# Splitting the last token tile of the last feed-forward into two halves of its output features

## Chip, cores and metric

One Trainium2 chip, one of its cores; the sets of experiments ran on three different chips, each with runs of the kernel before beside them. The metric is device microseconds of one execution; lower is better. Beside it I use a finer measure that comes from the traces: the time from the start of the last token tile's first matmul (called t = 0 in this document) to later points of the same execution. Two executions of the same program agree on it to a few ns as far as the end of computing, while whole times of one program scatter by 1 to 2 us (nine runs of the kernel before on one chip span 1.3 to 1.8).

## The reference, cut to what matters

A Conformer block on x of 2 x 4000 x 512: feed-forward, attention, convolution, a second feed-forward, and a final layer normalization. The change is in the last two lines:

```python
h = _layernorm(x3, axis=-1)
h = _silu(h @ w_ff2_a) @ w_ff2_b      # 512 -> 2048 -> 512
x4 = x3 + 0.5 * h
return _layernorm(x4, axis=-1)
```

## The kernel before

Tokens come in 16 chunks of 500, a chunk in four tiles (TPC = 4) of 125 tokens. The second product of the feed-forward has for each tile 16 matmuls (FC = 16), whose stationary operand is a 128 x 125 block of activations and whose moving operand is a 128 x 512 block of weights; they accumulate in one bank of PSUM, the accumulator memory. In the last chunk the four tiles are done one after the other, so that each tile's epilogue (residual, statistics, normalization, store) runs while TensorE is at the next tile. The last tile has no next one.

```python
def ff_last(self, c, old):
    ...                                     # first product of all 16 blocks
    sl = self.nxt("ln", self.LN_SLOTS)
    for ti in range(TPC):
        for f in range(FC):
            self.ff_second(f, ti, *blocks[f], f == FC - 1)        # 128x125 by 128x512, PE
        self.residual(self.Yb[ti][0:TILE, :], self.b_Y[ti], c * TPC + ti, 0.5)   # DVE, reads PSUM
        self.ln_stats(c, sl, ti)                                  # DVE, bn_stats
        self.ln_mean(sl, ti)                                      # DVE, bn_aggr
        self.ln_factor(sl, ti)                                    # DVE add eps, then POOL power -0.5
        self.ln_norm(c, sl, ti, self.osb[0][:, ti, :], self.b_osb[0][ti], "DVE")
        self.store_out(c, self.osb[0], self.b_osb[0], ti, ti + 1, ("SP", "ACT"))  # 80 and 45 rows
```

Every operation goes through a helper that notes which buffers it reads and writes and puts the semaphore waits in front of it; a `Buf` stands for what is tracked as one. The program uses semaphores as counters: an operation that is done adds one to its engine's, and an engine that needs the result waits for that value. The order in which the program lists VectorE's operations is the order in which the traces show them (e1_order below tests it: there residual 1, listed earlier, starts at t = 1.95 instead of 3.02). In the lines of the profile PE is TensorE and PEld its weight loads, DVE is VectorE, POOL is GpSimd, ACT is ScalarE, and SPq is the queue of SyncE.

Of the kernel before, what the change touches and what calls it, by code (L numbers as in the profile page):

```python
# [8 lines left out]
ALU = mybir.AluOpType  # L9
# [3 lines left out]
B, T, D, F, KW = 2, 4000, 512, 2048, 3  # L13
TILE = 125
CHUNK = 500
TPC = CHUNK // TILE
# [6 lines left out]
FC = F // 128  # L23
# [195 lines left out]
class Conformer:  # L219
# [484 lines left out]
    def ff_last(self, c, old):  # L704

        S, late = self.S, FC - self.NP
        blocks = []
        for f in range(FC):
            if f < late:
                blocks.append((self.late[f], self.b_late[f]))  # L710
            else:
                s = self.nxt("P", self.NP)
                blocks.append((self.P[s], self.b_P[s]))
            self.ff_first(c, f, *blocks[f])
            self.pop({0: old // 2, 1: old - old // 2}.get(f, 0))
            self.tick()
        while self.later:
            self.tick()
        sl = self.nxt("ln", self.LN_SLOTS)
        for ti in range(TPC):  # L720
            for f in range(FC):
                self.ff_second(f, ti, *blocks[f], f == FC - 1)
            self.residual(self.Yb[ti][0:TILE, :], self.b_Y[ti], c * TPC + ti, 0.5)
            self.ln_stats(c, sl, ti)
            self.ln_mean(sl, ti)
            self.ln_factor(sl, ti)
            self.ln_norm(c, sl, ti, self.osb[0][:, ti, :], self.b_osb[0][ti], "DVE")
            self.store_out(c, self.osb[0], self.b_osb[0], ti, ti + 1, ("SP", "ACT"))
# [720 lines left out]
```

## Time and profile before

| | before |
|---|---|
| device time, median of 4 runs | 2061.34 us (2060.94 to 2062.01) |
| span in the profile | 2056.9 us |
| TensorE busy | 2044.4 us |
| t = 0 (first matmul of the last tile) | at 2047.75 us |
| last matmul ends | t = 3.62 |
| aggregate of the last tile ends | t = 5.29 |
| normalization ends | t = 6.56 |
| end of the span | t = 9.20 |

The table reads as follows: nothing but the 5.58 us from 3.62 to 9.20 lies open behind TensorE, and 2.64 of these are the last store. Two more lines of before matter later, and neither was used in the prediction. First the page's row of instruction fetches (packets, MB, share of the DMA engines), then, from the waits of SyncE over the last microseconds (total us, times, longest), its wait for the stores to land:

```profile
q8 instruction: 77, 1.26, 0.3%
```
```profile
SPq L178 <- DMA out_dram<-work: 1.3, 2, 0.9
```

### The profile page before, as it was taken

What the parts mean: (1) busy time and instruction counts of PE and PEld (TensorE: products, weight loads), DVE (VectorE), ACT (ScalarE), POOL (GpSimd) and SP (SyncE); (2) the same over time, 40 slices, a digit from 0 to 9 for tenths busy, and PEclk for the clock granted to TensorE, in tenths of its full rate; (3) what the DMA queues carried; (4) which work ended last, traced back from release to release, by engine and by line L of the source; (5) the groups of instructions that cost most, each with busy time, mean ns of one, the idle gap of its engine ahead of it and who ended that gap; (6) DMA issues with size and microseconds to landing.
All of it is one profiled execution on the core that took longest, in us unless ns stands there. A gap on an engine that the chain in (4) does not pass through costs nothing.

```text
span 2056.9 us, 24335 instructions
## 1 busy us (share of the span) xinstructions
PE 2044.4 (99%) x9625; PEld 1036.1 (50%) x9625; DVE 1111.3 (54%) x2274; ACT 744.6 (36%) x1270; POOL 128.1 (6%) x275
## 2 busy tenths in 40 slices
PE   9999999999999999999999999999999999999998
PEld 4555555554444444444444444444445555555554
DVE  4245444325556667666666676667764443443443
ACT  3433333333333333333333333333345443443432
POOL 2011100000000000000000000000011000000000
PEclk9999999999999999999999999999999999999999
DMA  7222221110000100014301000101143111111111
GB/s 178 56 61 56 58 61 49 46 49 11 16 6 23 24 16 18 21 23 110 92 17 24 18 23 14 23 18 24 39 127 93 31 31 41 31 31 41 31 31 42
DMA packets 209323, 87.71 MB, mean 43 GB/s; under 512 B 157873, under 2 KB 208692, under 8 KB 209204
## 3 DMA queue, kind: packets, MB, share of 16 engines
q1 hardware_dynamic: 208808, 85.79, 16.7%
q8 instruction: 77, 1.26, 0.3%
q14 instruction: 42, 0.34, 0.1%
q10 hardware_dynamic: 396, 0.31, 0.0%
HBM read 29.53 MB, written 19.04 MB: 24 GB/s over the span
## 4 chain that ended last, share of the span: by engine, by line
PE 96%; DVE 2%; SPq 1%; DMA 1%; issue 0%; POOL 0%; ACT 0%; POOLq 0%; DVEq 0%; ACTq 0%
PE s L465 54%; PE y L465 42%; SPq L515 1%; DMA xt<-in_x_dram 1%; DMA work<-in_dw_dram 0%; DVE work L547 0%; SPq L511 0%; DVE work L569 0%; DVE wff L1048 0%; DVE xt L667 0%; SPq L519 0%; POOL work L661 0%; POOL work L1057 0%; DVE wff L953 0%; ACT work L507 0%
## 5 line engine op out<-in xcount | busy, mean ns | idle before, releaser
L507 ACT ACTIVATE work<-s 128x500 bf16<-128x500 f32 (+2 forms) x1063 | 623.7, 587 | 1220.4 <-PE s L465 1218.9
L465 PE MATMUL s<-work,wff 128*128 128x500 bf16 x2560 | 627.7, 376 | 1.7 <-DVE work L504 1.7
L465 PE MATMUL s<-work,keys 128*128 128x500 bf16 x2048 | 517.5, 374 | 0.1
L465 PE MATMUL y<-work,keys 128*128 128x500 bf16 x2048 | 514.4, 373 | 0.1
L465 PE MATMUL y<-wff,work 128*125 128x512 bf16 x2016 | 506.6, 379 | 0.0
L820 DVE TENSOR_TENSOR work<-work 128x500 f32<-128x500 f32 x496 | 334.8, 675 | 281.9 <-ACT work L507 279.1
L465 PEld LDWEIGHTS s<-work,wff 128*128 128x128 bf16 x2560 | 250.1, 98 | 280.9 <-issue 1.8
L465 PEld LDWEIGHTS y<-wff,work 128*125 128x125 bf16 x2016 | 275.2, 137 | 173.5
L465 PEld LDWEIGHTS y<-work,keys 128*128 128x128 bf16 x2048 | 199.2, 97 | 234.4 <-DVE work L885 1.1
L465 PEld LDWEIGHTS s<-work,keys 128*128 128x128 bf16 x2048 | 199.8, 98 | 232.2 <-DVE work L749 0.6
L667 DVE SCALAR_TENSOR_TENSOR xt<-y,xt 125x512 bf16<-125x512 f32 x128 | 79.8, 684 | 342.0 <-PE y L465 342.0
L547 DVE BATCH_NORM_STATS2 work<-xt 125x6 f32<-125x512 bf16 x316 | 199.8, 681 | 10.4 <-DMA xt<-in_x_dram 10.2
L556 POOL TENSOR_TENSOR work<-work 125x4 f32<-125x4 f32 x76 | 77.0, 1013 | 1116.6 <-DVE work L554 1116.6
L465 PE MATMUL s<-work 128*125 128x512 bf16 (+3 forms) x528 | 133.7, 378 | 2.2 <-DVE work L1158 1.2
L569 DVE TENSOR_SCALAR work<-xt,work 125x512 bf16<-125x512 bf16 x279 | 113.0, 449 | 16.5 <-POOL work L556 12.9
L667 DVE SCALAR_TENSOR_TENSOR xt<-s,xt 125x512 bf16<-125x512 f32 x56 | 38.8, 692 | 146.3 <-PE s L465 146.3
L465 PEld LDWEIGHTS s<-work 128*125 128x125 bf16 (+2 forms) x528 | 70.5, 135 | 48.1 <-issue 2.7
L667 DVE SCALAR_TENSOR_TENSOR xt<-s,work,xt 125x512 bf16<-125x512 f32 x64 | 48.1, 751 | 32.5 <-PE s L465 31.9
L465 PE MATMUL s<-keys,work 128*128 128x500 bf16 x256 | 64.4, 376 | 0.0
L957 DVE SCALAR_TENSOR_TENSOR wff<-wff,s 128x500 bf16<-128x500 f32 x57 | 38.6, 678 | 43.5 <-PE s L465 41.4
L507 ACT ACTIVATE wff<-s 128x500 f32<-128x500 f32 x67 | 39.2, 587 | 57.2 <-PE s L465 55.1
L507 ACT ACTIVATE work<-keys,work 128x500 bf16<-128x500 bf16 x64 | 50.5, 795 | 1.1 <-DVE work L1062 1.1
(90 smaller groups left out, 491.4 us busy)
## 6 DMA issues: line engine op xcount, KB each, us to landing
xt<-in_x_dram SPq DMA_DIRECT2D x15, 500.0 KB
out_dram<-work SPq DMA_DIRECT2D x15, 500.0 KB
dcvd<-wff SPq DMA_DIRECT2D x52, 125.0 KB, 1.7
keys<-dcvd SPq DMA_DIRECT2D x13, 500.0 KB, 4.3
wff<-in_w_ff_a_dram SPq DMA_DIRECT2D x16, 256.0 KB, 4.7
keys<-work SPq DMA_DIRECT2D x8, 512.0 KB, 3.6
keys<-keys SPq DMA_DIRECT2D x32, 128.0 KB, 2.1
work<-work SPq DMA_TRANSPOSE x210, 2.5
```

What stands on the lines that cost most here:

```text
L465: self.S.op("PE", lambda e: e.matmul(out, lhsT, rhs, start=start, stop=stop), reads=reads, writes=[bank], inc=stop if inc is None else inc)
L507: return self.S.op("ACT", lambda e: e.activation(out, in_, func, **kw), reads=reads, writes=writes)
L515: return self.S.dma("SP", k, lambda e: e.dma_start_transpose(dst, src), reads=reads, writes=writes)
L547: self.S.op("DVE", lambda e: e.bn_stats(self.st[sl][:, ti, :], x), reads=[b_x], writes=[self.b_st[sl][ti]])
L556: S.op("POOL", lambda e: e.tensor_tensor(out=self.rs[sl], in0=self.va[sl], in1=self.neghalf[0:TILE, :], op=ALU.pow), reads=self.b_va[sl] + ...
L569: self.S.op("DVE", lambda e: e.tensor_scalar(out, x, self.mv[sl][:, ti, 0:1], self.rs[sl][:, ti:ti + 1], ALU.subtract, ALU.mult), reads=[b ...
L667: self.S.op("DVE", lambda e: e.scalar_tensor_tensor(out=self.XT[g], in0=ps, scalar=scalar, in1=self.XT[g], op0=ALU.mult, op1=ALU.add), rea ...
L820: S.op("DVE", lambda e, p=p: e.tensor_tensor(out=self.acc[s], in0=self.acc[s], in1=self.P[p], op=ALU.add), reads=[self.b_P[p], self.b_acc[ ...
L957: self.S.op("DVE", lambda e: e.scalar_tensor_tensor(out=out, in0=self.th[k], scalar=1.0, in1=ps[:, 0:CHUNK], op0=ALU.add, op1=ALU.mult), r ...
```

## The change

The intent: half of the last tile's residual and statistics need only half of the output features. If these are made first, VectorE can do that half while TensorE makes the other. The first half goes to tile 0's bank, which is free by then (in the trace of before it was read out by 2041.74, 6.0 us ahead of t = 0).

```diff
-        for ti in range(TPC):
+        for ti in range(TPC - 1):
             ...                                  # as before for tiles 0 to 2
+        ti = TPC - 1
+        g, x = c * TPC + ti, self.XT[c * TPC + ti]
+        st, b_st = self.st[sl][:, ti - 1:ti + 1, :], self.b_st[sl][ti - 1:ti + 1]
+        for n in range(2):
+            d = slice(n * D // 2, (n + 1) * D // 2)
+            ps, b_ps = self.Yb[(0, ti)[n]], self.b_Y[(0, ti)[n]]
+            for f, (p, b_p) in enumerate(blocks):
+                self.mm(ps[0:TILE, d], p[:, ti * TILE:(ti + 1) * TILE], self.Wb[:, f, d], f == 0, f == FC - 1,
+                        [self.b_Wb[f], b_p], b_ps)
+            S.op("DVE", lambda e, d=d, ps=ps: e.scalar_tensor_tensor(
+                out=x[:, d], in0=ps[0:TILE, d], scalar=0.5, in1=x[:, d], op0=ALU.mult, op1=ALU.add),
+                reads=[b_ps, self.bx[g]], writes=[self.bx[g]])
+            S.op("DVE", lambda e, d=d, n=n: e.bn_stats(st[:, n, :], x[:, d]), reads=[self.bx[g]], writes=[b_st[n]])
+        S.op("DVE", lambda e: e.bn_aggr(self.mv[sl][:, ti, :], st.rearrange("p t s -> p (t s)")),
+             reads=b_st, writes=[self.b_mv[sl][ti]])
+        ...                                      # factor, normalization and store as before
```

More of the change, by code (lines that the diff above doesn't have):

```diff
@@ L725, in ff_last @@
             self.ln_mean(sl, ti)
+            self.ln_factor(sl, ti)
+            self.ln_norm(c, sl, ti, self.osb[0][:, ti, :], self.b_osb[0][ti], "DVE")
+            self.store_out(c, self.osb[0], self.b_osb[0], ti, ti + 1, ("SP", "ACT"))
+        ti = TPC - 1
[13 more added lines that the diff above has]
+             reads=b_st, writes=[self.b_mv[sl][ti]])
+        for ti in (ti,):
             self.ln_factor(sl, ti)
```

## The prediction

> **What bounds the kernel now.** I read the page first, for the engine that sets the time.
>
> ```profile
> PE 2044.4 (99%) x9625; PEld 1036.1 (50%) x9625; DVE 1111.3 (54%) x2274; ACT 744.6 (36%) x1270; POOL 128.1 (6%) x275
> ...
> PE 96%; DVE 2%; SPq 1%; DMA 1%; issue 0%; POOL 0%; ACT 0%; POOLq 0%; DVEq 0%; ACTq 0%
> ```
>
> TensorE is busy for 2044.4 of 2056.9 us and makes up 96% of the chain that ended last. The change touches neither the number of multiplications nor anything before the last token tile; it can only shorten the little that TensorE does not cover. So the next view is the timeline of the end, from the last tile's first matmul (columns: start, duration, engine, line, operation, out<-in, count, idle time before and who ended it):
>
> ```profile
> 2047.75 1.89 PE L465 MATMUL y<-wff,keys 128*125 128x512 bf16 x8
> ...
> 2047.95 0.69 DVE L667 SCALAR_TENSOR_TENSOR xt<-y,xt 125x512 bf16<-125x512 f32 x1 [0.54 <-PE y L465]
> 2048.68 0.69 DVE L547 BATCH_NORM_STATS2 work<-xt 125x6 f32<-125x512 bf16 x1
> ...
> 2049.41 0.18 DVE L654 BATCH_NORM_AGGREGATE work<-work 125x2 f32<-125x6 f32 x1
> 2049.48 1.89 PE L465 MATMUL y<-wff,work 128*125 128x512 bf16 x8
> 2049.62 0.15 DVE L659 TENSOR_SCALAR work<-work 125x1 f32<-125x1 f32 x1
> 2049.86 0.55 POOL L661 TENSOR_TENSOR work<-work 125x1 f32<-125x1 f32 x1 [2.89 <-DVE work L659]
> 2050.44 0.41 DVE L569 TENSOR_SCALAR work<-xt,work 125x512 bf16<-125x512 bf16 x1 [0.66 <-POOL work L661]
> 2051.41 0.69 DVE L667 SCALAR_TENSOR_TENSOR xt<-y,xt 125x512 bf16<-125x512 f32 x1 [0.55 <-PE y L465]
> 2052.13 0.69 DVE L547 BATCH_NORM_STATS2 work<-xt 125x6 f32<-125x512 bf16 x1
> 2052.86 0.18 DVE L654 BATCH_NORM_AGGREGATE work<-work 125x2 f32<-125x6 f32 x1
> 2053.08 0.15 DVE L659 TENSOR_SCALAR work<-work 125x1 f32<-125x1 f32 x1
> 2053.31 0.55 POOL L661 TENSOR_TENSOR work<-work 125x1 f32<-125x1 f32 x1 [2.91 <-DVE work L659]
> 2053.89 0.41 DVE L569 TENSOR_SCALAR work<-xt,work 125x512 bf16<-125x512 bf16 x1 [0.66 <-POOL work L661]
> ```
>
> The last matmul's result is there at 2051.37 (49.48 + 1.89). What follows is serial: residual (2051.41), statistics, their aggregate (ends at 2053.04), variance plus epsilon, the power on GpSimd, the normalization (ends at 2054.31), and then the store, up to 2056.9. That is 5.5 us behind the last matmul, of which the change aims at the 1.42 us from 2051.41 to 2052.83: half of each of two operations. The reader should also see the first half of the excerpt: the same chain of tile 2 runs **under** tile 3's matmuls, and VectorE ends it with the normalization at 2050.44 to 2050.85. VectorE then idles 0.55 us.
>
> A third view, the groups of instructions kept apart by shape, has the rows that I use as prices (columns: count, busy us, mean ns of one, idle before):
>
> ```profile
> L465 PE MATMUL y<-wff,keys 128*125 128x512 bf16 x32 | 7.6, 379 | 0.0
> ...
> L480 PE MATMUL s<-work 125*128 125x125 bf16 x16 | 1.4, 220 | 1.1 <-ACT work L507 1.1
> ```
> ```profile
> 1525.16 0.57 PE L465 MATMUL s<-work 128*125 128x1 bf16 x8
> ```
> ```profile
> L957 DVE SCALAR_TENSOR_TENSOR wff<-wff,s 128x500 bf16<-128x500 f32 x57 | 38.6, 678 | 43.5 <-PE s L465 41.4
> ...
> L1055 DVE BATCH_NORM_AGGREGATE work<-wff 128x2 f32<-128x21 f32 x3 | 0.7, 249 | 0.1
> ```
> ```profile
> 1905.03 2.48 DVE L667 SCALAR_TENSOR_TENSOR xt<-y,xt 125x512 bf16<-125x512 f32 x4 [7.23 <-PE y L465]
> ```
>
> [...]eight matmuls start at 2047.75 and the next eight at 2049.48, 216 ns each.[...]in the excerpt at 1525.16, eight matmuls with 125 weight columns each and one moving column take 0.57 us, the last of them lasting 0.197, so they start every (0.57 - 0.20) / 7 = 53 to 58 ns, weight load included.[...]the change takes tile 0's bank, which was read out by 2041.74. No new wait comes from that.[...]
>
> **TensorE, part by part.** Removed: 16 matmuls of 512 columns, 16 weight loads. Added: 32 of 256 columns and 32 loads, as every half needs all 16 stationary blocks again. The dearest question is the pitch. [...]the measured pitch of loads is at most 58 ns, so I take 109 ns. A matmul's record: 379 ns at 512 columns, about 219 at 125, thus 0.41 ns per column, and 379 - 256 x 0.41 = 273 at 256. First half: 2047.75 + 15 x 0.109 + 0.273 = 2049.66. Second half: 2047.75 + 31 x 0.109 + 0.273 = 2051.40, against 2051.37 before. Cost on TensorE: **+0.04 us**[...].
>
> **VectorE, part by part.** Removed: one residual and one statistics of 512 (692 and 695 ns). Added: two of each at 256. The 500-wide row costs 678 against 692, about 1.1 ns per element[...]; so I take 692 - 256 x 1.04 = **425 ns** for each of the four. Their sum, 1.70 us, is 0.31 us more than before: each operation has about 0.16 us that doesn't shrink. The aggregate reads 12 values instead of 6; 6 take 183 ns and 21 take 249, so about 210, **+0.03 us**.
>
> What lies beside other work is decided by VectorE's order, in which I chose to compare the two built kernels: the first half's residual stands **behind** tile 2's normalization, which waits for GpSimd until 2050.44 and ends at 2050.85. So although its matmuls are done at 2049.66, it can't start before that. An operation without a wait on its predecessor starts some 0.08 us before that one's end is recorded (four residuals of 0.68 take 2.48, not 2.73); one with a wait starts 0.03 us after it (2048.64 to 2048.68). Hence:
> - residual 1: 2050.77 to 2051.20
> - statistics 1: 2051.23 to 2051.65
> - residual 2, which waits for statistics 1, since both use the same row buffer, and for the matmuls (2051.40, past): 2051.69 to 2052.11
> - statistics 2: 2052.15 to 2052.57
> - aggregate of 12: 2052.61 to 2052.82, against 2053.04 before.
>
> From there all is as before: power, normalization, store. The sum is **-0.22 us**, that is 2061.27 - 0.22 = 2061.05 us, 0.01% of the whole.
>
> **Rivals.** (a) *VectorE's order does not matter*, the intended gain: residual and statistics of the first half wholly under the second's matmuls. Then the end is 2051.44 + 0.425 + 0.034 + 0.425 + 0.034 + 0.21 = 2052.57, a gain of 0.47 us: 2060.8. Against it stands the normalization of tile 2 at 2050.44 and the in-order sequence. (b) *Weight loads pace the halved matmuls*. The load's record is 136 ns, longer than 109; if the pitch were 136, the second half would end at 2047.75 + 31 x 0.136 + 0.273 = 2052.24, and the aggregate 1.16 us later (the four terms of (a) plus 0.04 of wake-up), 2053.40: a loss of 0.36 us, 2061.6. If a load were to start only after the previous matmul had streamed[...], the loss would be 1.26 us: 2062.5. The row of one-column matmuls speaks against both, and the 216 ns at 512, where 136 ns of load vanish. (c) *Nothing to be measured*: the three runs of before lie between 2060.94 and 2062.01, five times my effect.
>
> **Range and chances.** The whole chain behind the last matmul is 5.5 us, 0.27% of the time, so no outcome of the change reaches 2% (41 us)[...]. The center is 2061.05. Rival (a) would make 2060.8, (b) 2061.6 to 2062.5, and the runs scatter by about half a us to either side; so 2059.9 to 2062.4 should hold it. Faster by over 2%: 0.003; within 2%: 0.994; slower: 0.003.
>
> **What would show it.** In the changed profile: 32 matmuls of 256 columns whose groups of eight start 0.87 us apart (109 ns each); 1.09 or more would mean that loads pace them. The first residual of tile 3 begins at the end of tile 2's normalization, not at the end of its own matmuls, and VectorE's idle time of 0.55 us there is gone. Four operations of about 425 ns with no gap but 0.03 us; if they are nearer 350 the gain is 0.4. An aggregate of about 0.21, and 3.8 us from its end to the end of the span, as before. I would be wrong if the pitch is over 115 ns, if VectorE took the first residual ahead of tile 2's normalization, or if the double wait of residual 2 costs more than 0.1 us.

## The result, and the profile after

The changed kernel took 2061.59 us (median of 4 runs, 2060.75 to 2061.99), before 2061.34. The ratio is 1.000, with a 95% interval of 0.9983 to 1.0018. Ratios here are taken over fast runs; they are not quite the ratio of the medians that I quote. All runs compared were in the fast state (granted clock 0.998 to 1.000), or single runs of unknown state, which I use for their traces only.

The timeline of the end, after the change, without the weight loads:

```profile
2047.94 1.04 PE L465 MATMUL y<-wff,keys 128*125 128x256 bf16 x8
...
2048.82 1.04 PE L465 MATMUL y<-wff,work 128*125 128x256 bf16 x8
...
2050.56 1.04 PE L465 MATMUL y<-wff,work 128*125 128x256 bf16 x8
2050.64 0.41 DVE L569 TENSOR_SCALAR work<-xt,work 125x512 bf16<-125x512 bf16 x1 [0.67 <-POOL work L661]
2050.96 0.42 DVE L739 SCALAR_TENSOR_TENSOR xt<-y,xt 125x256 bf16<-125x256 f32 x1
2051.41 0.43 DVE L742 BATCH_NORM_STATS2 work<-xt 125x6 f32<-125x256 bf16 x1
2051.88 0.42 DVE L739 SCALAR_TENSOR_TENSOR xt<-y,xt 125x256 bf16<-125x256 f32 x1
2052.34 0.43 DVE L742 BATCH_NORM_STATS2 work<-xt 125x6 f32<-125x256 bf16 x1
2052.80 0.21 DVE L743 BATCH_NORM_AGGREGATE work<-work 125x2 f32<-125x12 f32 x1
...
2053.86 0.41 DVE L569 TENSOR_SCALAR work<-xt,work 125x512 bf16<-125x512 bf16 x1 [0.66 <-POOL work L661]
```

The reader should see four things. Groups of eight halved matmuls start 0.87 us apart, 109 ns each. The first residual of the last tile (2050.96) follows the normalization of tile 2, although its own matmuls were done at 2049.85. From there VectorE has no idle time but 0.03 us a step, and the second residual (2051.88) does not wait for TensorE, which ended at 2051.60. The four operations take 416 to 429 ns.

Here t = 0 is at 2047.94, 0.19 us later than before; this has nothing to do with the change. Measured from t = 0, the aggregate ends at 5.07 instead of 5.29, and the normalization at 6.33 instead of 6.56: **0.23 us earlier, as predicted (0.22)**. But the end of the span is at 9.00 instead of 9.20 here and at 9.10 in a second profile of the changed kernel. From the end of the normalization to the end of the span it takes 2.67 and 2.77 us, where before took 2.64 and 2.59. So part of the gain is lost in the store. The two lines of before have changed to:

```profile
q8 instruction: 78, 1.28, 0.3%
```
```profile
SPq L178 <- DMA out_dram<-work: 1.3, 1, 1.3
```

There is one more instruction fetch, and the wait for the stores, which came in two pieces of which the longer was 0.9, is one of 1.3. The last section of the experiments comes back to this.

### The profile page after: what moved, and what is told of

Read it like the earlier page. It is cut to its first block, busy times and chain, and to the rows that moved or that the text cites. A ratio compares the mean times of both kernels' runs of the same rounds, so it can differ in the third digit from the quotient of the medians.

```text
span 2056.9 us, 24370 instructions
## 1 busy us (share of the span) xinstructions
PE 2044.7 (99%) x9641; PEld 1037.7 (50%) x9641; DVE 1112.5 (54%) x2276; ACT 745.0 (36%) x1270; POOL 127.8 (6%) x275
## 4 chain that ended last, share of the span: by engine, by line
PE 96%; DVE 2%; SPq 1%; DMA 1%; POOL 0%; issue 0%; ACT 0%; POOLq 0%; DVEq 0%; ACTq 0%
PE s L465 54%; PE y L465 42%; SPq L515 1%; DMA xt<-in_x_dram 1%; DVE work L547 0%; DMA work<-in_dw_dram 0%; DVE work L569 0%; DVE wff L1068 0%; SPq L511 0%; DVE xt L667 0%; SPq L519 0%; POOL work L661 0%; POOL work L1077 0%; DVE wff L973 0%; ACT work L507 0%
## 5 line engine op out<-in xcount | busy, mean ns | idle before, releaser
L465 PE MATMUL y<-wff,work 128*125 128x512 bf16 (+1 forms) x2024 | 506.8, 378 | 0.0
```

The source lines that it names most:

```text
L465: self.S.op("PE", lambda e: e.matmul(out, lhsT, rhs, start=start, stop=stop), reads=reads, writes=[bank], inc=stop if inc is None else inc)
```

## The experiments

My theory: VectorE's order sets the gain, matmuls at half width are still paced by their own streaming, and the second bank is needed. Rivals: loads pace the matmuls, or the gain is bound elsewhere. The table has all kernels; times in us from t = 0, unless noted. "Store" is from the end of the normalization to the end of the span. "Last fetch" is when the last 16 KiB packet of queue q8 ran, counted from the end of the normalization; I read it from the DMA packets in the trace.

| kernel | t = 0 at | last matmul ends | aggregate ends | normalization ends | store | end of span | last fetch |
|---|---|---|---|---|---|---|---|
| before | 2047.75 | 3.62 | 5.29 | 6.56 | 2.64 | 9.20 | -1.99 to -0.74 |
| before, again | 2047.92 | 3.62 | 5.29 | 6.56 | 2.59 | 9.15 | -1.99 to -0.74 |
| after | 2047.94 | 3.66 | 5.07 | 6.33 | 2.67 | 9.00 | 0.04 to 1.29 |
| after, again | 2047.96 | 3.66 | 5.06 | 6.33 | 2.77 | 9.10 | 0.33 to 1.34 |
| matmuls alone | 2049.84 | 3.66 | 5.33 | 6.60 | 2.63 | 9.22 | -0.22 to 0.82 |
| vector alone | 2047.77 | 3.62 | 5.71 | 6.97 | 2.54 | 9.52 | -2.27 to -1.20 |
| one bank | 2047.89 | 5.45 | 6.69 | 7.96 | 3.09 | 11.05 | 0.58 to 1.59 |
| quarters | 2047.87 | 3.84 | 5.52 | 6.79 | 2.59 | 9.38 | 1.59 to 2.77 |
| eighths | 2048.81 | 7.50 | 9.17 | 10.44 | 4.00 | 14.44 | 1.01 to 2.64 |
| row halves | 2048.28 | 3.66 | 4.93 | 6.19 | 2.80 | 8.99 | 0.32 to 1.52 |
| order | 2048.28 | 3.66 | 4.90 | 6.16 | 2.84 | 9.01 | 0.31 to 1.50 |
| order, row halves | 2048.49 | 3.66 | 4.83 | 6.09 | 2.90 | 9.00 | 0.46 to 1.47 |
| uneven | 2049.18 | 3.66 | 4.77 | 6.03 | 3.51 | 9.54 | 0.88 to 2.14 |
| uneven, row halves | 2048.04 | 3.66 | 4.69 | 5.96 | 3.84 | 9.80 | 1.01 to 2.46 |

All kernels gave correct results.

### VectorE's order (e1_order)

```diff
-            self.ln_norm(... tile 2 ...); self.store_out(... tile 2 ...)     # ahead of the first half
+            if n == 0: ln_norm and store_out of tile 2                      # behind the first half's statistics
```

> The change, with tile 2's normalization and store put behind the first half's residual and statistics in VectorE's order. All times are from the start of tile 3's first matmul to the end of tile 3's aggregate; before it took 5.29 us, after the change 5.07. Theory (VectorE's order holds back the first half): residual 1 starts at 1.95 instead of 3.02, residual 2 then waits for its matmuls alone (3.69), the aggregate ends at 4.82, a gain of 0.25 over the change and 0.47 over before. Rival (something else holds it back, such as the second half's matmuls or the bank): stays at 5.07. In the whole time no difference beyond the scatter of 0.5 us is expected from either, perhaps 2060.9.

```profile
2048.28 1.04 PE L465 MATMUL y<-wff,keys 128*125 128x256 bf16 x8
...
2050.22 0.42 DVE L740 SCALAR_TENSOR_TENSOR xt<-y,xt 125x256 bf16<-125x256 f32 x1
...
2051.03 0.40 DVE L569 TENSOR_SCALAR work<-xt,work 125x512 bf16<-125x512 bf16 x1
```

Measured: residual 1 starts at t = 1.95, as expected, and the aggregate ends at 4.90, 0.17 before the change's 5.07. So the order is what held back the first half. It missed the expected 4.82 by 0.07, because residual 2 started at 3.76 and not at 3.69. Whole time: 2061.02 (5 runs), before 2060.83, ratio 1.000 (0.9986 to 1.0013): nothing to be seen, as expected.

### The double wait (e10_order_row_halves)

In e1_order residual 2 waits for two engines: for TensorE (its matmuls) and for VectorE itself (statistics 1, which reads the same row buffer). The new buffers track the two halves of the row apart, so that residual 2 needs no wait for statistics 1.

```diff
+        b_half = [Buf("x half") for _ in range(2)]        # start with the state of self.bx[g]
-                reads=[b_ps, self.bx[g]], writes=[self.bx[g]])
+                reads=[b_ps, b_half[n]], writes=[b_half[n]])
```

> e1_order with the row's halves tracked apart, so that residual 2 waits for the matmuls alone. In e1_order it started 106 ns after the last matmul's end, against 37 ns for a residual that waits for the matmuls alone. Theory (the second semaphore costs about 70 ns when the matmuls come last, because the wait for them is an instruction of its own ahead of the residual): starts at 3.69 instead of 3.76 us, aggregate ends at 4.83 instead of 4.90. Rival (the 70 ns belong to the halved matmuls or to the order): 3.76 and 4.90 again.

The timeline of e1_order and that of this kernel, around residual 2:

```profile
2050.90 1.04 PE L465 MATMUL y<-wff,work 128*125 128x256 bf16 x8
...
2052.04 0.42 DVE L740 SCALAR_TENSOR_TENSOR xt<-y,xt 125x256 bf16<-125x256 f32 x1 [0.61 <-PE y L465]
```
```profile
2051.11 1.04 PE L465 MATMUL y<-wff,work 128*125 128x256 bf16 x8
...
2052.18 0.42 DVE L743 SCALAR_TENSOR_TENSOR xt<-y,xt 125x256 bf16<-125x256 f32 x1 [0.55 <-PE y L465]
```

From the start of the last eight matmuls to residual 2 it takes 1.14 us in the first and 1.07 in the second. The aggregate ends at 4.83, as expected. So the second semaphore costs 0.07 us when the matmuls come last. The traces of the change and of e1_order have a wait as an instruction of its own (EVENT_SEMAPHORE, 21 ns long) ahead of residual 2, and that of e10 has none. In the change it cost nothing visible: it ran at t = 3.70, before statistics 1 ended at 3.90. Whole time: 2061.38, before 2061.23.

### The wait through the shared row (e9_row_halves)

The same separate tracking, but in the changed kernel's own order.

> The change with the row's two halves tracked apart, so that residual 2 does not wait for statistics 1. Theory: residual 2 starts 0.08 us before the recorded end of statistics 1 instead of 0.03 after it, aggregate at 4.95 instead of 5.07 us. If the wait costs nothing: 5.07.

```profile
2051.75 0.43 DVE L745 BATCH_NORM_STATS2 work<-xt 125x6 f32<-125x256 bf16 x1
2052.09 0.41 DVE L742 SCALAR_TENSOR_TENSOR xt<-y,xt 125x256 bf16<-125x256 f32 x1
```

Measured: residual 2 starts at 3.81 instead of 3.93, the aggregate ends at 4.93 (expected 4.95). The wait for statistics 1, which runs just before, costs 0.12 us here: 0.08 of overlap that is lost and 0.03 of waking up.

### Each side alone (e2_matmuls_alone, e3_vector_alone)

```diff
# e2: 32 matmuls of 256 into one bank, no read between them
-            residual and statistics of 256, twice
+        self.residual(ps[0:TILE, :], b_ps, c * TPC + ti, 0.5); self.ln_stats(c, sl, ti); self.ln_mean(sl, ti)
```

> Only TensorE's part of the change: 32 matmuls of 256 columns into one bank, then one residual and one statistics of 512 as before. Theory (weight loads are hidden under 256 columns, pitch 109 ns): last matmul ends 3.65 us after the first one's start instead of 3.62, aggregate ends at 5.33 instead of before's 5.29: it costs 0.035 us. Rival (loads pace them at 136 ns): 4.49 and 6.17.

```diff
# e3: matmuls as before, VectorE in halves
+        for f in range(FC): self.ff_second(f, ti, *blocks[f], f == FC - 1)
         for n in range(2):
-            for f, (p, b_p) in enumerate(blocks): self.mm(... half n ...)
```

> Only VectorE's part of the change: 16 matmuls of 512 columns as before, then residual and statistics in two halves each, nothing beside matmuls. Theory (each half operation keeps about 0.16 us that does not shrink): four operations of 0.425 us and three gaps of 0.034, aggregate at 5.70 instead of before's 5.29: it costs 0.41 us. Rival (operations halve with their width): 5.03 to 5.1.

Measured: the matmuls alone end at 3.66 and cost 0.04 us (5.33 for 5.29), so loads do not pace them. VectorE's split alone costs 0.41 us (5.71 for 5.29). These are the prices that the change pays. Its gain of 0.23 is what the overlap brings, less these.

### The bank (e4_one_bank)

```diff
-            ps, b_ps = self.Yb[(0, ti)[n]], self.b_Y[(0, ti)[n]]
+            ps, b_ps = self.Yb[ti], self.b_Y[ti]
```

> The change with both halves in the same accumulator bank. Theory (the other bank is needed: the second half's matmuls must wait until the first half has been read out): TensorE stands still from 1.75 to about 3.49 us, its last matmul ends at 5.40, the aggregate at 6.56, 1.5 us later than after the change. Rival (the bank does not matter because VectorE is late anyway): 5.07.

```profile
2051.39 1.09 PE L465 MATMUL y<-wff,keys 128*125 128x256 bf16 x8 [1.58 <-DVE xt L739]
```

TensorE stands still for 1.58 us, until the first half's residual has read the bank (the second half starts at 2051.39, t = 3.50), and the aggregate ends at 6.69, 1.62 us after the change's. Expected was 6.56; the rest is the double wait (0.07) and 0.05 in the first eight matmuls, which take 1.09 instead of 1.04. So the choice of tile 0's bank is worth more than the change gains. The wait is the one that the helper puts in front of the matmuls; what happens without it was not tried.

### When do weight loads pace TensorE? (e5_quarters, e6_eighths)

e2 with four and eight parts in place of two.

```diff
-        for n in range(2):
+        for n in range(4):      # 8 in e6
```

> The disputed cost by itself, at 128 columns: 64 matmuls of 128 columns with 64 weight loads into one bank, then one residual and one statistics of 512. Theory (a load of 125 columns takes the array 58 ns, hidden as long as the matmul streams longer): [...]load 58.3, so 58.3 ns each; last matmul ends at 63 x 0.0583 + 0.22 = 3.89 us, aggregate at 5.57 (before 5.29). Rival (a load is exposed for its whole record of 136 ns): 8.8 and 10.5.

> The same at 64 columns: 128 matmuls and 128 loads. Theory: the loads pace them at 58.3 ns whatever the width, last matmul ends at 127 x 0.0583 + 0.19 = 7.6 us, aggregate at 9.28, 4.0 us later than before, and the whole time 2065.3. Rival (matmul width still sets the pitch[...]): 3.9 and 5.6, whole time 2061.6.

From the timeline of the eighths:

```profile
2050.16 0.62 PE L465 MATMUL y<-wff,work 128*125 128x64 bf16 x8
...
2050.62 0.62 PE L465 MATMUL y<-wff,keys 128*125 128x64 bf16 x8
```

Eight matmuls of 64 columns each take 0.46 us, 57.5 ns each, and in the quarters the pitch is 57.5 too ((3.84 - 0.22) / 63). If the width alone set the pitch, 64 columns would take half of that: an estimate, on the straight line through 216 ns at 512 and 109 at 256 columns, is 29 ns (with it the rival's last matmul ends at 127 x 0.029 + 0.19 = 3.9), and the very first two matmuls of the eighths do start 28 ns apart. On the same line lie 320 columns (135 to 136 ns) and 192 (82 to 83 ns, both e12 and e14 below); it gives 55.5 at 128, where 57.5 was measured. So I put 57.5 ns down to a load of 125 columns, though the record of a load lasts 138 ns in the eighths (mean): it is hidden at 256 columns and at 192, and paces the matmuls at 128 and 64. Last matmuls end at 3.84 and 7.50, expected 3.89 and 7.6. The eighths' aggregate is 3.88 us later than before's. The whole time, however, was 2066.24 (4 runs) against 2061.18, so 5.1 us later; ratio 1.0022 (1.0007 to 1.0038). The profile has its missing microsecond in the store: 4.00 us instead of 2.64.

### The shortest chain (e12_uneven_only, e14_uneven_row_halves), and controls (e13_before_again, e15_after_again)

Behind the last matmul only the second part counts, so it may be the smaller one.

```diff
-            d = slice(n * D // 2, (n + 1) * D // 2)
+            d = slice((0, 320)[n], (320, D)[n])
```

> e1_order with 320 and 192 columns in place of 256 and 256. Theory (behind the last matmul only the second part's residual and statistics count, 0.36 us each at 192): matmuls end at 3.66, residual 2 starts at 3.70, aggregate ends at 4.69 us, 0.13 under e1_order's 4.82 and 0.60 under before. Rival (192-column matmuls paced by loads of 136 ns): 5.5. The whole time: 2060.7, hardly apart from the scatter.

> e12_uneven_only (320 and 192 columns, order changed) with the row's parts tracked apart, the shortest chain of all. Theory: residual 2 starts at 3.69, aggregate ends at 4.70 us, normalization at 5.96, 0.60 us under before's 6.56. In the whole time: e12_uneven_only came out 0.7 us above before although its chain was 0.53 shorter; if that was scatter of the start, this one is at or below before, around 2060.7; if something in it slows the kernel elsewhere, it is above again.

> The kernel before, unchanged, submitted as if it were a new one: what five runs of the same program scatter to. Aggregate of tile 3 at 5.29 us after the first matmul's start, exactly. Theory (the differences of whole times seen so far arise in the first 55 us and in the landing of the last store, not in the change): its whole time differs from the other runs of before by up to 0.5 us in the median, and its last tile starts anywhere from 2047.7 to 2049.9. Rival (an identical program gives an identical start): 2047.75 again, medians within 0.1 us.

> The changed kernel again, five runs on the same chip as the other three. Chain as the first time: residual 1 at 3.02, residual 2 at 3.93, aggregate at 5.07 us. Whole time within the scatter of before's: theory -0.23 us plus or minus 0.4.

The chains came out as expected: 4.77 (expected 4.69, with the double wait's 0.07) and 4.69 (expected 4.70). The normalization of e14 ends at 5.96, 0.60 us before that of the kernel before. But neither is faster. e12: 2061.92 against 2061.18, ratio 1.0002 (0.9988 to 1.0016). In another set of runs, with nine runs of before at 2061.23: e14 2061.52, e15 (the change) 2061.72, e13 (before) 2061.13. None of these differences is clear of the scatter. But the median of every kernel with the overlap that had runs of its own (the change twice, e1, e10, e12, e14) lies above that of before in the same set, by 0.15 to 0.74 us, and five of the six means do: whole times show no gain, and whether they hide a small loss stays open. The two controls: e13's chain ended at 5.29 as expected, with t = 0 at 2047.92 (0.17 us from the first profile of before) and its median 0.10 us from the other runs of before, so that its whole time does not tell the theory from the rival. e15's chain came out as expected (3.02, 3.93, 5.06), but its whole time, 0.49 us above before, missed the expected -0.23 plus or minus 0.4. In the profile of e14 the end of the span is 0.60 us **later** than before's, counted from t = 0: the chain gains 0.60, the store takes 3.84 instead of 2.64.

```profile
2051.73 0.36 DVE L743 SCALAR_TENSOR_TENSOR xt<-y,xt 125x192 bf16<-125x192 f32 x1
...
2052.52 0.21 DVE L750 BATCH_NORM_AGGREGATE work<-work 125x2 f32<-125x12 f32 x1
...
2053.58 0.41 DVE L569 TENSOR_SCALAR work<-xt,work 125x512 bf16<-125x512 bf16 x1 [0.67 <-POOL work L661]
```
```profile
SPq L178 <- DMA out_dram<-work: 2.4, 1, 2.4
```

Both fences are of e14: its timeline, and SyncE's wait for the stores, 2.4 us in one piece against 1.3 in two.

### Where the gain goes: an instruction fetch in the store's way

The last column of the table goes with the store column. The store has 125 packets of 1 KiB, which start 0.89 us after the end of the normalization and end by 1.6 if nothing is in the way. In the kernels whose last fetch ends before the store starts (before, twice; vector alone; matmuls alone, at 0.82) or starts when nearly all of the store has run (quarters, 1.59), the last store packet ends at 1.58 or 1.59, and the store column has 2.54 to 2.64. In all others the fetch overlaps it, and the store column has 2.67 to 4.00, by and large the more, the later the fetch ends. e14 shows it packet by packet: 117 of its 125 packets start by 1.56 us, and the last eight start at 2.45 to 3.13, the first of them 0.01 us from the fetch's end at 2.46. In e12 it is eight again, from 2.14 to 2.80, with the fetch's end at 2.14. In the three longest stores (e14, e12 and the eighths) eight packets come late; in the others that the fetch overlaps the delay is smaller. Eight packets (five of SyncE's 80, three of ScalarE's 45) are one sixteenth of the store, and the profile's page counts 16 DMA engines: my estimate is that they are the share of the one engine that ran the fetch. The records do not name the engine; I conclude it from the number and the times. A second queue of fetches, q14, is no rival: in all 14 profiles, those of before too, it has one packet of 8 KiB between 0.45 and 1.08 and one between 1.44 and 1.88 after the normalization.

Whose fetch is it? In the trace of before each of the 77 packets of q8 has 16 KiB. From one of them to the next TensorE starts 256 matmuls, loads and other instructions in the median (243 to 271 for the middle four fifths), VectorE 36. 77 times 256 are 19,712, and TensorE has 9625 matmuls and as many loads, 19,250. So I take q8 for the queue of TensorE's instructions, an estimate from these counts. The two one-sided kernels confirm it, with their rows of the page, first e3 (VectorE alone changed), then e2 (TensorE alone changed):

```profile
q8 instruction: 77, 1.26, 0.3%
```
```profile
q8 instruction: 78, 1.28, 0.3%
```

So the 32 instructions that the change adds to TensorE's stream (16 matmuls and 16 loads) bring one more fetch (the quarters and eighths, which add 96 and 224, have 78 too). With it the last one moves from 4.57 to between 6.4 and 6.7 us after t = 0, to just where the store begins. By then TensorE has finished the last matmul; what this last fetch holds, the profile does not show. A shorter chain then moves the store further into it. What is shown is that each profile in which the fetch overlaps the store has the delay and each without has not; that the fetch causes it is argued from this and from the late packets. Not tried is the direct test, to shift the fetch alone (for instance by 16 matmuls fewer in the program's `warm(18)` at the start) and keep the chain of e14. Why this fetch comes some 0.3 to 0.5 us later in the uneven kernels (6.9 to 7.0) is open too.

## Why the prediction was right

- **Time.** 2061.59 measured, 2061.05 predicted, inside 2059.9 to 2062.4. That tells little: the range is wide enough for the scatter alone, and holds rival (a), (c) and most of (b) too. In the medians the change is even 0.25 above before, where -0.22 was forecast. The predicted -0.22 us cannot be seen in whole times: five runs of the unchanged kernel span 2060.54 to 2062.19 (e13). It can be seen in the trace: -0.23.
- **Pitch of 109 ns, loads hidden, +0.04 on TensorE.** Right: 109 ns, last matmul at 3.66 (predicted 3.65), and e2 costs 0.04. The 109 was my estimate: the trace of before shows 216 ns at 512 columns, half of which is 108, and none at 256. The load's price of 53 to 58 ns, taken from a corner of the kernel with one-column matmuls, was confirmed at 57.5 by the quarters and eighths. (The sum that the prediction shows gives only the 53, a mean that holds one short gap of 28 ns; the other gaps in those records are 58 to 59 ns.)
- **425 ns for each half operation, 210 for the aggregate.** Right: 416 to 429, and 211. The slope of 1.04 ns per element was my estimate; the trace of before has 14 ns between 500 and 512 columns (678 and 692), about 1.2 each. Measured afterwards, the residual took 691 ns at 512 and 416 to 425 at 256, which is 1.04 to 1.07, and the statistics 695 and 428 to 429, which is 1.04.
- **VectorE's order.** Right: residual 1 at t = 3.02 (predicted 2050.77 - 2047.75 = 3.02), residual 2 at 3.93 (3.94). Rival (a), an order that does not matter, was excluded by the change's own trace and made true by e10: there the gain is the 0.46 us that (a) forecast at 0.47.
- **Rival (b)**, loads that pace, is excluded at 256 columns (109 ns), and e5 and e6 show it at 128 and 64 (57.5 ns). Its second form, with 2062.5, was an estimate: half of 216 ns and 58 ns for the load make 166 ns for each matmul, a loss of 1.3 us.
- **The step that failed: "From there all is as before: power, normalization, store."** Power and normalization were; the store was not. It took 0.03 to 0.18 us more than in the two profiles of before, and 0.9 to 1.2 more for the shorter chains of e12 and e14. I had not looked at instruction fetches. The prediction also had this stretch too short: its own lines give 2056.9 - 2053.04 = 3.9 us from the aggregate's end to the end of the span, not the 3.8 that it names "as before"; after the change it was 3.93 and 4.04. It did not spoil the number only because the change's gain and this loss are both smaller than the scatter.
- **Rival (c)**, nothing to be measured, describes the result in whole times, and a large part of its cause can be named: t = 0 itself lies between 2047.75 and 2049.84 in these profiles, of programs that are equal up to there. When I align the traces, these differences all arise in the first 55 us, where the first inputs and weights come in, and stay constant to 0.03 us for the other 1990.

## What to carry to other kernels

Splitting a last operation in two to hide half of it pays the fixed part of each instruction twice (0.16 us here) and gains only if the engine that is to work beside is free at that time **in its own order** (0.23 us with the first half behind tile 2's normalization, 0.39 ahead of it in e1_order): look which operation stands ahead of it, and what that one waits for. When the remaining tail is a few microseconds, compare times from a common point in the trace, and look at what else uses the DMA engines at the end: in e12 and e14 the store that an extra fetch of instructions overlapped lost more than the split gained.
